# State space convolution and MLP on one core: turned products read on POOL's queue, four buffers for tile a, and a new order of the work

## The chip, the core and the metric

The program runs on one core of one Trainium2 chip. The core has five engines: PE (matrix products), DVE (VectorE), ACT (ScalarE), POOL (GpSimd) and SP, which here only issues transfers. Each engine works through its own instructions in their order; semaphores join them. SP and POOL both issue DMA transfers, and sixteen DMA engines move the bytes of either. The metric is the device time of one execution in microseconds (us): before the change 343.65 us, the median of 3 runs (342.4, 343.65 and 347.39).

## The reference

With `x` of 2048 positions and 512 channels, the reference computes `h = x + A(layernorm(x))` and returns `h + B(layernorm(h))`. A is a state space layer: a kernel `K` of 2048 taps per channel is built from 128 complex exponentials, and the sequence is convolved with it through an FFT of twice the length. B normalizes once more and is a two-layer MLP of width 1376 with gelu.

```python
def _A_ref(u, A_re, A_im, B_re, B_im, C_re, C_im, log_dt, Dskip):
    ...
    P = jnp.exp(logdA[:, :, None] * l[None, None, :])
    K = jnp.einsum("dn,dnl,dn->dl", Cc, P, dB).real
    ...
    Yf = Uf * Kf[None, :, :, :]
    y = (lambda x, s, axes=(-2,-1): jnp.fft.irfft2(x, s=s, axes=axes).astype(jnp.bfloat16))(Yf, (1, L2), axes=(-2, -1))[:, :, 0, :L]
    y = (lambda x, *d: x.transpose(*d))(y, 0, 2, 1) + u * Dskip[None, None, :]
...
x = A_u
h = x + _A_ref(_layernorm(x, axis=-1), A_A_re, A_A_im, A_B_re, A_B_im, A_C_re, A_C_im, A_log_dt, A_Dskip)
h2 = h + _B_ref(_layernorm(h, axis=-1), B_w1, B_b1, B_w2, B_b2)
```

## The kernel before

The kernel does the transforms as matrix products with tables that it makes itself, and works on the channels in two halves of 256 (`hh` is 0 or 1). Its stages, with the names that the profile shows:

- **Front.** POOL makes index rows (`si`, `ga`, `lf`, `wp`, `wq`), DVE and ACT make the layer's parameters (`psi`, `th`, `amp`, tiles `w`), ACT the sines of the tables (`M`, `base`) and the first exponentials (`Pt`, `Q`, written `<-th`). DVE takes the statistics of `x` (`st<-x`).
- **A stage** (`norm_in`): for each of 16 slices of `x` one normalized slice `u`, two products `aps<-u,BD` on PE, a cast `a<-aps` to bf16 on ACT or DVE, and a write `A_dram<-a` of 256 KB on SP. Tile `a` has two buffers. Four reads `X<-A_dram` of 1 MB each bring the result back in another order.
- **Exponentials times sines** (`p_half`, `q_half`): eight units p and ten units q for each half. A unit is a pair of products `pv` or `qv` on PE, a sine `s<-pv` or `sq<-qv` on ACT, and a product in place on DVE (`Pt<-s,Pt` or `Q<-sq,Q`).
- **Kernel taps** (`kgen`): four groups of 128 small products `kps<-Q,Pt` with as many weight loads on PE; a copy `ku` on ACT and two sums `near` and `far` on DVE after each group; then writes to `KD_near` and `KD_far` in DRAM and five reads `kt`, three on SP and two on POOL.
- **X stage** (`x_stage`): 16 units of eight products `xps<-X,M` and a cast back into `X`.
- **Convolution** (`conv`): eight steps for each half. A step is the spectrum of the taps, 22 products into `kfps` (lines 838 and 840), a cast `kf` on ACT, four DVE products `pa`, `pb`, then eight products `zps<-pa,R` on PE and a cast `z`. SP writes `z` to DRAM (`Zd<-z`, 256 KB, line 883). A read then turns it into `ZT` (`ZT<-Zd`, 256 KB in 16 rows of 16 KB, line 881). Tile `z` has three buffers, each free when its write has landed.
- **Weights** (`loads`): after the taps `kt` of the second half have come, POOL issues the loads of the MLP's weights and of `x` again (`w_r`, `w_sb`, `r`), 4.8 MB.
- **MLP** (`mlp`): it starts with four products `y<-ZT` (line 890) that need all turned products of the second half, then normalizes, and alternates `h1ps` and `o2ps` on PE with gelus on ACT to the end.

Each piece of work up to the MLP is recorded as an operation (`Sched.op`) with a list of those it depends on and a cost. A table of numbers, `ORDER`, found outside the program, says in which order the operations' instructions are written: an even number 2n is operation n on its first engine, an odd one on its second (a cast can go to ACT or DVE). The costs are not used when the program is built. So `ORDER` alone sets the order on each engine, on SP's and POOL's queues too; PSUM tiles have three buffers (`p`) and one (`q`, for `zps`). The MLP's order is that of its code.

The two lines that issue the write and the turned read of a convolution step are these:

```python
        def turn(k2=k2):
            nc.sync.dma_start(K.ZT[k2:k2 + 121:8, hh].rearrange("p h j d -> p (h j d)"), Zd[4 * k2:4 * k2 + 4].rearrange("f (q r) d -> (f q) (r d)", q=4))

        w = S.op("SP", 0.45, lambda cell=cell, ks=ks: nc.sync.dma_start(Zd[2 * ks.start:2 * ks.stop].rearrange("f p d -> p f d"), cell["zs"][:].rearrange("p k c d -> p (k c) d")), [e], rel=[e], lat=2.4)
        K.o_z.append(S.op("SP", 0.45, turn, [w, K.o_turn], lat=2.8))
```

Of the kernel before, what the change touches and what calls it, by code (L numbers as in the profile page):

```python
# [161 lines left out]
def prefix(nc0, S, K, cp, ct, c2):  # L162
# [36 lines left out]
    K.lf = ct.tile([P, 21], f32, name="lf")  # L199
    at = 0  # L200
    for base, n in ((256, 2), (511, 4), (1022, 7), (2044, 4), (1, 4)):
        count(nc0, K.lf[:, at:at + n], base, [[1, n]])
        at += n
# [487 lines left out]
def kgen(nc, S, K, cv, sc, psp, hh, KD):  # L691
# [40 lines left out]
    def gets():  # L732
        kt = K.kt[hh] = cv.tile([P, 5, HW], bf16, name="kt", tag="kt", bufs=2)
        for t in range(5):
            src = near[:].rearrange("(g k) r c -> (k r) g c", g=4)[128 * t:128 * t + 128] if t < 2 else far[t - 2].rearrange("(g k) r c -> (k r) g c", g=4)
            (nc.gpsimd if t % 2 else nc.sync).dma_start(kt[:, t, :].rearrange("p (g c) -> p g c", g=4), src)
# [431 lines left out]
```

## Time and profile before

| what | us |
|---|---|
| median of 3 runs | 343.65 |
| the profiled execution's own time | 341.9 |
| its span, first to last instruction | 340.1 |
| PE busy in the span | 253.5 |
| DVE busy | 203.8 |
| ACT busy | 188.0 |
| POOL busy | 32.6 |

The profile is of one execution. Times within it count from the start of its span; the 1.8 us between span and own time lie around it. A busy PE is not PE at its peak, since products overlap. In the tables by stretch, the columns are the stretch, its length, then for PE, PE's weight loads, DVE, ACT and POOL the busy time with the number of instructions in brackets, then the granted PE clock (1.00 is full), the busy share of the DMA engines and GB/s. SPq is SP's queue, "PEld" are weight loads, "issue" is time in which an engine waited for nothing that the profile shows.

### The profile page before, as it was taken

What the parts mean: (1) busy time and instruction counts of PE and PEld (TensorE: products, weight loads), DVE (VectorE), ACT (ScalarE), POOL (GpSimd) and SP (SyncE); (2) the same over time, 40 slices, a digit from 0 to 9 for tenths busy, and PEclk for the clock granted to TensorE, in tenths of its full rate; (3) what the DMA queues carried; (4) which work ended last, traced back from release to release, by engine and by line L of the source; (5) the groups of instructions that cost most, each with busy time, mean ns of one, the idle gap of its engine ahead of it and who ended that gap; (6) DMA issues with size and microseconds to landing.
All of it is one profiled execution on the core that took longest, in us unless ns stands there. A gap on an engine that the chain in (4) does not pass through costs nothing.

```text
span 340.1 us, 6070 instructions
## 1 busy us (share of the span) xinstructions
PE 253.5 (75%) x2408; PEld 155.3 (46%) x2422; DVE 203.8 (60%) x427; ACT 188.0 (55%) x308; POOL 32.6 (10%) x92
## 2 busy tenths in 40 slices
PE   4046984476674998998798978502689799999996
PEld 4012351242373775667666755401465344444443
DVE  3999995559981999989224443510727367274102
ACT  2799796479832999986143525420573263363440
POOL 8200007800000100000015000100000000000000
PEclk9655567579955899999599997965599999999999
DMA  6400007640156921111098964443000100100001
GB/s 180 175 2 0 4 18 195 201 147 0 65 166 169 245 67 31 45 49 35 4 239 225 337 230 125 123 124 93 0 2 0 46 17 15 47 2 31 31 11 52
DMA packets 29830, 30.18 MB, mean 89 GB/s; under 512 B 7113, under 2 KB 27594, under 8 KB 29418
## 3 DMA queue, kind: packets, MB, share of 16 engines
q1 hardware_dynamic: 27722, 23.03, 23.4%
q0 software_dynamic: 2080, 6.76, 6.4%
q8 instruction: 19, 0.31, 0.4%
q14 instruction: 9, 0.07, 0.1%
HBM read 18.58 MB, written 11.20 MB: 88 GB/s over the span
## 4 chain that ended last, share of the span: by engine, by line
PE 36%; DMA 24%; DVE 18%; ACT 12%; issue 6%; POOL 2%; SPq 1%; DVEq 0%; ACTq 0%; POOLq 0%
DMA Zd<-z 13%; PE h1ps L992 12%; PE o2ps L1004 9%; PE kps L704 5%; DMA A_dram<-a 5%; PE kfps L840 4%; DMA kt<-KD_far 3%; DVE st L761 3%; DVE Pt L70 3%; DMA KD_far<-far 2%; DVE w L70 2%; ACT a L80 2%; PE yps L974 2%; ACT y2T L80 2%; DVE Q L70 1%
## 5 line engine op out<-in xcount | busy, mean ns | idle before, releaser
L994 ACT ACTIVATE hT<-h1ps,b_sb 128x512 bf16<-128x512 f32 (+3 forms) x55 | 33.0, 603 | 28.0 <-PE h1ps L992 27.4
L992 PE MATMUL h1ps<-y2T,w_r 128*128 128x512 bf16 (+3 forms) x217 | 44.7, 350 | 2.3 <-ACT y2T L80 1.9
L840 PE MATMUL kfps<-kt,M 128*128 128x256 bf16 x320 | 42.2, 278 | 1.2 <-DMA kt<-KD_far 0.6
L1004 PE MATMUL o2ps<-w_sb,hT 128*128 128x512 bf16 (+3 forms) x183 | 39.2, 366 | 1.7 <-DVE ot L70 1.5
L840 PEld LDWEIGHTS <-M 128*128 128x128 bf16 x320 | 29.2, 99 | 10.1 <-issue 3.4
L992 PEld LDWEIGHTS <-w_r 128*128 128x128 bf16 (+1 forms) x220 | 23.0, 105 | 22.4 <-issue 4.9
L70 DVE TENSOR_TENSOR pa<-X,kf 128x1024 bf16<-128x1024 bf16 x16 | 11.1, 691 | 28.1 <-ACT kf L80 28.1
L1004 PEld LDWEIGHTS <-hT 128*128 128x128 bf16 (+1 forms) x187 | 18.1, 98 | 20.9 <-issue 1.8
L704 PE MATMUL kps<-Q,Pt 128*32 128x20 bf16 x1024 | 18.6, 221 | 11.2 <-issue 9.6
L70 DVE TENSOR_TENSOR ot<-o2ps,h_sb 128x512 bf16<-128x512 f32 (+1 forms) x13 | 8.4, 650 | 29.6 <-PE o2ps L1004 28.7
L80 ACT CAST kf<-kfps 128x1024 bf16<-128x1024 f32 x14 | 14.2, 1013 | 17.2 <-PE kfps L840 9.0
L704 PEld LDWEIGHTS <-Pt 128*32 128x32 bf16 x1024 | 17.9, 169 | 12.4 <-issue 10.5
L80 ACT CAST z<-zps 128x1024 bf16<-128x1024 f32 x15 | 15.3, 1023 | 13.6 <-DMA Zd<-z 12.8
L80 ACT CAST a<-aps 128x1024 bf16<-128x1024 f32 x15 | 15.0, 1033 | 12.2 <-DMA A_dram<-a 12.2
L70 DVE TENSOR_TENSOR Pt<-s,Pt 128x1024 bf16<-128x1024 bf16 x32 | 20.4, 691 | 1.2 <-ACT s L118 1.1
L118 ACT ACTIVATE sq<-qv 128x1024 bf16<-128x1024 int16 x20 | 20.3, 1072 | 0.0
L613 ACT ACTIVATE Pt<-th 128x256 bf16<-128x256 f32 x64 | 20.3, 405 | 0.0
L80 ACT COPY y2T<-tps 128x512 bf16<-128x512 bf16 x16 | 8.5, 584 | 17.6 <-PE tps L984 17.6
L405 POOL DMA_DIRECT2D Dp<-Dd x24 | 13.0, 546 | 43.7 <-DMA Dd<-ds 42.1
L70 DVE TENSOR_TENSOR h_sb<-yps,r 128x512 f32<-128x512 f32 x12 | 8.3, 689 | 14.8 <-PE yps L974 14.8
L777 PE MATMUL aps<-u,BD 128*128 128x512 bf16 x30 | 11.0, 473 | 8.0 <-DVE u L772 5.3
L118 ACT ACTIVATE s<-pv 128x1024 bf16<-128x1024 int16 x16 | 16.6, 1064 | 0.0
(224 smaller groups left out, 470.9 us busy)
## 6 DMA issues: line engine op xcount, KB each, us to landing
A_dram<-a SPq DMA_DIRECT2D x16, 256.0 KB, 3.0
X<-A_dram SPq DMA_DIRECT2D x4, 1024.0 KB, 6.0
Zd<-z SPq DMA_DIRECT2D x16, 256.0 KB, 3.4
ZT<-Zd SPq DMA_DIRECT2D x16, 256.0 KB, 3.4
...
out_dram<-ot SPq DMA_DIRECT2D x15, 128.0 KB, 1.7
...
```

Of the source, the lines that this page charges most:

```text
L70: nc.vector.tensor_tensor(out, a, b, op)
L80: nc.scalar.copy(out, in_)
L118: nc.scalar.activation(out, v.bitcast(i16)[..., 0:2 * n:2], ACT.Sin, scale=S2PI / 65536)
L405: nc.gpsimd.dma_start(t[o::128 // cnt], bass.AP(row.tensor, row.offset + 1024 * kh, [[0, cnt], [1, 1024]]))
L613: nc.scalar.activation(K.Pt[:, k, 1, :], K.th[:, ds], ACT.Exp, scale=float(8 * k))
L704: nc.tensor.matmul(kps[32 * g:32 * g + 32, i // 8, at:at + 20], lhsT=Pt[:, :, u, c], rhs=Q[:, :, u, c], start=True, stop=True, tile_positi ...
L761: o = S.op("DVE", 2.9, roots, deps=[S.op("DVE", 0.62, lambda j=j: nc.vector.bn_stats(st[:, j, :], x[:, j, :]), [here]) for j in range(16)])
L777: nc.tensor.matmul(ps[:, h, :], lhsT=K.BD[:, h].rearrange("p a b -> p (a b)"), rhs=cell["u"][:], start=True, stop=True)
L840: nc.tensor.matmul(ps[:, k, c, :], lhsT=K.M[:, t, 2 * k2 + k, c, :], rhs=kt[:, t, :], start=(c == 1 and t == 0), stop=(t == 4))
L992: nc.tensor.matmul(pt[:fs, 0:n], lhsT=K.w1_sb[:, dc, fc * P:fc * P + fs], rhs=y2T[tb][:, dc, js, :].rearrange("p a b -> p (a b)"), start=( ...
L994: nc.scalar.activation(hT[tb % 2][:fs, fc, cols], pt[:fs, 0:n], ACT.Gelu_apprx_tanh, bias=K.b1_sb[:fs, fc:fc + 1], scale=1.0)
L1004: nc.tensor.matmul(pt[:], lhsT=h[:fs, fc, jj * P:(jj + 1) * P], rhs=K.w2_sb[:fs, fc, d], start=(fc == 0), stop=(fc == NFC - 1))
```

## The change

The turned reads `ZT<-Zd` go out on POOL's queue instead of SP's. Tile `a` gets four buffers instead of two. The small rows for the table phases are made differently: POOL makes three rows `si` in f32 instead of six in bf16, and five small ACT instructions turn them, `ga` and `kf` into the bf16 rows, where DVE made three of these before; `lf` is made earlier on POOL. The bookkeeping of the operations is extended: a transfer is now two operations, its issue on SP or POOL and a "DMA" operation that issues nothing, so operation numbers shift. The costs are changed, which the built program doesn't use. `ORDER` is another table: the new numbers give another order on PE, ACT, DVE, POOL and SP up to the end of the convolution. The MLP is untouched.

```diff
 ORDER = [
-    106, 250, 0, 2, 20, 22, 4, 24, 26, 16, 192, 30, 28, 36, 34, 38, 144, 32, 62, 140, 40, 148, 152, 64, 156, 278, 82, 272, 44, 84, 268, 138, 274, 54, 276, 108, 258, 126, 252,
+    110, 4, 24, 28, 8, 32, 38, 6, 40, 196, 36, 136, 126, 124, 66, 132, 112, 42, 148, 68, 122, 138, 134, 22, 114, 130, 128, 116, 168, 304, 120, 70, 140, 118, 144, 164, 290,
...
+    def dma(self, eng, cost, fn, deps, size, rel=(), acq=None, lat=2.2):
+        i = self.op(eng, cost, fn, deps, acq)
+        return self.op("DMA", size, None, [i], None, rel, lat)
...
-    si = c2.tile([1, 6, P], bf16, name="si")
+    si = c2.tile([1, 3, P], f32, name="si")
+    sb = c2.tile([1, 2, 3, P], bf16, name="sb")
...
+        count(nc0, si[:, n], 1, pattern)
         for m in range(2):
-            count(nc0, si[:, 2 * n + m], 1 - 128 * m, pattern)
-            R[nm + "m" * m] = si[:, 2 * n + m]
+            R[nm + "m" * m] = sb[:, m, n]
...
-    ts(nc, R["k"][:], kf[0:1, :], 1.0 / 128, ALU.mult)
-    for m, div in enumerate((8192, 64)):
-        ts(nc, gb[:, m], ga[:], 1.0 / div, ALU.mult)
-    K.o_rows = S.op("DVE", 0.4, nc.vector.split(nc0.vector), [K.o_bits])
+
+    def rows():
+        nc0.scalar.activation(R["k"][:], kf[0:1, :], ACT.Copy, scale=1.0 / 128)
+        for m, div in enumerate((8192, 64)):
+            nc0.scalar.activation(gb[:, m], ga[:], ACT.Copy, scale=1.0 / div)
+        for m in range(2):
+            nc0.scalar.activation(sb[:, m], si[:], ACT.Copy, bias=-128.0 * m)
...
         def out(e, cell=cell):
-            cell["a"] = lp.tile([P, 2, 512], bf16, name="a", tag="a", bufs=2)
+            cell["a"] = lp.tile([P, 2, 512], bf16, name="a", tag="a", bufs=4)
             evac(nc, e, cell["a"][:], cell["p"][:])
...
         def turn(k2=k2):
-            nc.sync.dma_start(K.ZT[k2:k2 + 121:8, hh].rearrange("p h j d -> p (h j d)"), Zd[4 * k2:4 * k2 + 4].rearrange("f (q r) d -> (f q) (r d)", q=4))
+            nc.gpsimd.dma_start(K.ZT[k2:k2 + 121:8, hh].rearrange("p h j d -> p (h j d)"), Zd[4 * k2:4 * k2 + 4].rearrange("f (q r) d -> (f q) (r d)", q=4))
```

What the new table moves is shown at three places. The first is SP's queue from the end of the taps of the second half on. `Zd0` and `Zd1` are the two halves' products in DRAM, `z_...` the buffers. Before:

```order
L729 DMA KD_near1_67<-near_2304 128x512
L730 DMA KD_far1_66<-far_2305 128x3x256
L881 DMA ZT_2585<-Zd0_68 16x8192 x2
L883 DMA Zd0_68<-z_2627 128x4x256
L736 DMA kt_2656<-KD_near1_67 128x4x64
L736 DMA kt_2656<-KD_far1_66 128x4x64 x2
L881 DMA ZT_2585<-Zd0_68 16x8192
L883 DMA Zd0_68<-z_2686 128x4x256
L881 DMA ZT_2585<-Zd0_68 16x8192
L883 DMA Zd0_68<-z_2770 128x4x256
L881 DMA ZT_2585<-Zd0_68 16x8192
L883 DMA Zd1_69<-z_2814 128x4x256
```

SP's queue after, from the same place:

```order
L741 DMA KD_near1_67<-near_2145 128x512
L742 DMA KD_far1_66<-far_2146 128x3x256
L895 DMA Zd0_68<-z_2580 128x4x256
L895 DMA Zd0_68<-z_2617 128x4x256
L748 DMA kt_2620<-KD_near1_67 128x4x64
L748 DMA kt_2620<-KD_far1_66 128x4x64 x2
L895 DMA Zd0_68<-z_2686 128x4x256
L895 DMA Zd0_68<-z_2770 128x4x256
L895 DMA Zd1_69<-z_2814 128x4x256
L895 DMA Zd1_69<-z_2858 128x4x256
```

Before, every write stands behind the read of the write ahead of it; after, only writes and the taps' transfers are left. The reads now stand on POOL's queue, around the taps `kt` of the second half and the loads of the weights. POOL after:

```order
L748 DMA kt<-KD_near_65 128x4x64
L748 DMA kt<-KD_far_64 128x4x64
L893 DMA ZT<-Zd_68 16x8192 x4
L748 DMA kt<-KD_near_67 128x4x64
L748 DMA kt<-KD_far_66 128x4x64
L893 DMA ZT<-Zd_68 16x8192 x2
L1131 COPY gate<-kt 128x1
L932 DMA w_r_2697<-in_B_w_dram 128x4x1376
```

POOL after, from the last of the weights' loads on:

```order
L1136 DMA r_2709<-in_A_u_dram 128x6144
L1137 CAST b_sb<-b_bf 128x11
L893 DMA ZT<-Zd_68 16x8192 x2
L893 DMA ZT<-Zd_69 16x8192 x8
L959 MEMSET hT_3109 1x512
```

Four turned reads of the first half stand ahead of the two taps' reads that POOL issues; the last two of the first half and all of the second stand behind the loads.

The second place is SP's queue around the taps of the first half. Before:

```order
L798 DMA X<-A_dram 128x8x512
L418 DMA M<-Bd 1x64x128 x2
L798 DMA X<-A_dram 128x8x512
L729 DMA KD_near_65<-near 128x512
L730 DMA KD_far_64<-far 128x3x256
L798 DMA X<-A_dram 128x8x512
L736 DMA kt<-KD_near_65 128x4x64
L736 DMA kt<-KD_far_64 128x4x64 x2
L798 DMA X<-A_dram 128x8x512
```

SP after:

```order
L810 DMA X<-A_dram 128x8x512 x4
L741 DMA KD_near_65<-near 128x512
L742 DMA KD_far_64<-far 128x3x256
L430 DMA M<-Bd 1x64x128 x2
L748 DMA kt<-KD_near_65 128x4x64
L748 DMA kt<-KD_far_64 128x4x64 x2
```

All four reads of X now stand ahead of the taps' writes. The third place is ACT from the A stage into the sines of the first half (`a<-aps` are the A stage's casts, `u` its normalized slices, `s` and `sq` the sines, `ku` the copy after a group of kernel taps). Before:

```order
L80 CAST a<-aps 128x1024
L586 CAST M<-w_210 128x32x16
L501 CAST M<-psi_202 128x16x32
L80 CAST a<-aps 128x1024 x4
L770 ACTIVATE u<-x,mv,r1y 128x512
L80 CAST a<-aps 128x1024
L118 ACTIVATE s<-pv 128x1024 x2
L118 ACTIVATE sq<-qv 128x2x32x16
```

ACT after:

```order
L80 CAST a<-aps 128x1024
L118 ACTIVATE s<-pv 128x1024
L598 CAST M<-w_208 128x32x16
L118 ACTIVATE s<-pv 128x1024 x3
L782 ACTIVATE u<-x,mv,r1y 128x512
L80 CAST a<-aps 128x1024
L80 COPY QL<-lps 128x2048
L118 ACTIVATE s<-pv 128x1024
L118 ACTIVATE sq<-qv 128x2x32x16
L118 ACTIVATE sq<-qv 128x8x8x16
L118 ACTIVATE sq<-qv 128x2x32x16 x4
L118 ACTIVATE sq<-qv 128x8x8x16
```

Before, eleven of ACT's fifteen casts `a` stand ahead of the first sine `s`; after, three of its nine do, and the rest lie between the sines. DVE makes seven of the sixteen casts after, one before.

More of the change, by code (lines that the diff above doesn't have):

```diff
@@ L179, in prefix @@
     count(nc0, kf[:], 0, [[1, 64]])
+    K.lf = ct.tile([P, 21], f32, name="lf")
+    at = 0
+    for base, n in ((256, 2), (511, 4), (1022, 7), (2044, 4), (1, 4)):
+        count(nc0, K.lf[:, at:at + n], base, [[1, n]])
+        at += n
+    start = S.op("POOL", 2.6, None)
     K.ones = cp.tile([P, P], bf16, name="ones")
@@ L198, in prefix @@
             R[f"{nm}{1 << n}"] = gb[:, m, n]
[L199 to L203, printed above, removed]
+    table = S.op("POOL", 2.6, None, [start])
     split = ((3, 15), (0, 7), (0, 1), (1, 1), (4, 1))
@@ L226, in prefix @@
     K.bw = bw
-    K.o_bits = S.op("DVE", 1.6, nc.vector.split(nc0.vector))
+    K.o_bits = S.op("DVE", 1.5, nc.vector.split(nc0.vector), [start])
     R["k"] = c2.tile([1, 64], bf16, name="row_k")
-    ts(nc, R["k"][:], kf[0:1, :], 1.0 / 128, ALU.mult)
-    for m, div in enumerate((8192, 64)):
-        ts(nc, gb[:, m], ga[:], 1.0 / div, ALU.mult)
-    K.o_rows = S.op("DVE", 0.4, nc.vector.split(nc0.vector), [K.o_bits])
+    def rows():
[4 more added lines that the diff above has]
+            nc0.scalar.activation(sb[:, m], si[:], ACT.Copy, bias=-128.0 * m)
+    K.o_rows = S.op("ACT", 1.5, rows, [table])
     mask = c2.tile([P, 8], bf16, name="mask")
@@ L267, in outer @@
             count(nc, wq[p0:p1, at:at + cnt], base, pattern + [[0, 2]])
-    pl = S.op("POOL", 6.0, lambda: None)
+    pl = S.op("POOL", 4.4, None, [K.o_rows])
     def make():
@@ L389, in tables @@
     d = S.op("DVE", 1.35, dirichlet, [f])
-    w = S.op("SP", 0.7, lambda: nc.sync.dma_start(Dd[:].rearrange("r p l -> p r l"), ds[:].rearrange("p a r l -> p (a r) l")), [d], lat=2.5)
+    w = S.dma("SP", 0.55, lambda: nc.sync.dma_start(Dd[:].rearrange("r p l -> p r l"), ds[:].rearrange("p a r l -> p (a r) l")), [d], 0.3)
     b = S.op("DVE", 1.5, last_row, [f])
-    wb = S.op("SP", 0.7, lambda: nc.sync.dma_start(Bd[:].rearrange("r p l -> p r l"), bs[:].rearrange("p t c l -> p (t c) l")), [b], lat=2.5)
+    wb = S.dma("SP", 0.55, lambda: nc.sync.dma_start(Bd[:].rearrange("r p l -> p r l"), bs[:].rearrange("p t c l -> p (t c) l")), [b], 0.3)
     sums = []
@@ L411, in mul @@
                        cell["t"][:].rearrange("p (k b f) -> p k b f", k=8, f=k2), ALU.mult)
-            x = S.op("POOL", 2.0 if n < 4 else 7.0, spread, [w] + K.o_free, acq=DT[n], lat=2.5)
-            sums.append(S.op("DVE", 1.23, mul, [x, bases[n, 0]] + K.o_src, rel=[x]))
+            x = S.dma("POOL", 1.1 if n < 4 else 4.4, spread, [w] + K.o_free, 0.8, acq=DT[n])
+            sums.append(S.op("DVE", 1.23, mul, [x, bases[n, 0]] + K.o_src, rel=[x - 1]))
     def put_rows():
@@ L418, in put_rows @@
             nc.sync.dma_start(K.M[127:128, 1:5, :, c, :], Bd[c:8:2].rearrange("t (k h) l -> t k (h l)", k=16).unsqueeze(0))
-    K.o_tab = S.op("SP", 1.4, put_rows, sums + [wb, K.o_m[1]], lat=2.5)
+    K.o_tab = S.dma("SP", 1.4, put_rows, sums + [wb, K.o_m[1]], 0.2)
     S.group = "turned"
@@ L455, in tr @@
                 T[nm] = ps[:, n, :]
-        arrive = S2("LOAD", 0.85, lambda: None, [arrive] if arrive is not None else [])
+        arrive = S2("LOAD", 0.85, None, [arrive] if arrive is not None else [])
         Z[pair[0]] = S2("PE", 1.75, tr, [arrive], acq="p", bias=300)
@@ L717, in out @@
                     stt(nc, o[:, :, d], v[:, a, :], K.half_sign[:], cell["u"][:, a], ALU.mult, ALU.add)
-            m = S.op("PE", 2.6, mms, K.o_p[s] + K.o_q[s], acq="p")
+            m = S.op("PE", 2.15, mms, K.o_p[s] + K.o_q[s], acq="p")
             mm.append(m)
@@ L736, in gets @@
             (nc.gpsimd if t % 2 else nc.sync).dma_start(kt[:, t, :].rearrange("p (g c) -> p g c", g=4), src)
-    p = S.op("SP", 2.0, puts, ends, rel=[ends[0]], lat=3.0)
-    K.o_kt[hh] = S.op("SP", 1.0, gets, [p], lat=3.0, acq="kt")
+    p = S.dma("SP", 1.4, puts, ends, 0.6, rel=[ends[0]], lat=2.4)
+    K.o_kt[hh] = S.dma("SP", 1.6, gets, [p], 0.6, acq="kt", lat=2.6)
 def norm_in(nc, S, K, lp, psp, x, A_dram):
@@ L758, in roots @@
         stt(nc, mv[:, :, 1], mv[:, :, 0], -1.0, K.rs[:], ALU.mult, ALU.mult)
-    here = S.op("XLOAD", 13.5, lambda: None)
+    here = S.op("XLOAD", 13.5, None)
     o = S.op("DVE", 2.9, roots, deps=[S.op("DVE", 0.62, lambda j=j: nc.vector.bn_stats(st[:, j, :], x[:, j, :]), [here]) for j in range(16)])
@@ L785, in norm_in @@
         a = S.op(("ACT", "DVE"), (0.94, 1.2), out, [m], acq="a", rel=[m])
-        K.o_a.append(S.op("SP", 0.7, lambda cell=cell, j=j: nc.sync.dma_start(A_dram[:, :, j, :], cell["a"][:]), [a], rel=[a], lat=2.5))
+        K.o_a.append(S.dma("SP", 0.55, lambda cell=cell, j=j: nc.sync.dma_start(A_dram[:, :, j, :], cell["a"][:]), [a], 0.78, rel=[a]))
 def x_load(nc, S, K, A_dram, change, gate):
@@ L798, in load @@
             nc.sync.dma_start(K.X[:].rearrange("p k c d -> p (k c) d")[:, ks], av[:, ks])
-        K.o_xl.append(S.op("SP", 1.0 if n else 1.2, load, K.o_xl[-1:] if n else K.o_a + gate, lat=3.5 + 2.5 * n))
+        K.o_xl.append(S.dma("SP", 0.5, load, [K.o_xl[-1] - 1] if n else K.o_a + gate, 2.95))
 def x_stage(nc, S, K, psp, hh):
@@ L871, in conv @@
         S.group = f"kf{hh}"
-        p = S.op("PE", 4.8, spectrum, [K.o_kt[hh], K.o_tab, K.o_m[1], K.o_top, K.o_r] + [K.o_x[hh][k2]] + back_ops[max(k2 - 2, 0):k2 - 1], acq="p", rel=[K.o_kt[hh]], bias=-1.0 * k2)
+        p = S.op("PE", 4.8, spectrum, [K.o_kt[hh], K.o_tab, K.o_m[1], K.o_top, K.o_r] + [K.o_x[hh][k2]] + back_ops[max(k2 - 2, 0):k2 - 1], acq="p", rel=[K.o_kt[hh] - 1], bias=-1.0 * k2)
         f = S.op(("ACT", "DVE"), (1.0, 1.2), out, [p], acq="kf", rel=[p], bias=-1.0 * k2)
@@ L880, in turn @@
         def turn(k2=k2):
-            nc.sync.dma_start(K.ZT[k2:k2 + 121:8, hh].rearrange("p h j d -> p (h j d)"), Zd[4 * k2:4 * k2 + 4].rearrange("f (q r) d -> (f q) (r d)", q=4))
-        w = S.op("SP", 0.45, lambda cell=cell, ks=ks: nc.sync.dma_start(Zd[2 * ks.start:2 * ks.stop].rearrange("f p d -> p f d"), cell["zs"][:].rearrange("p k c d -> p (k c) d")), [e], rel=[e], lat=2.4)
-        K.o_z.append(S.op("SP", 0.45, turn, [w, K.o_turn], lat=2.8))
+            nc.gpsimd.dma_start(K.ZT[k2:k2 + 121:8, hh].rearrange("p h j d -> p (h j d)"), Zd[4 * k2:4 * k2 + 4].rearrange("f (q r) d -> (f q) (r d)", q=4))
+        w = S.dma("SP", 0.5, lambda cell=cell, ks=ks: nc.sync.dma_start(Zd[2 * ks.start:2 * ks.stop].rearrange("f p d -> p f d"), cell["zs"][:].rearrange("p k c d -> p (k c) d")), [e], 0.85, rel=[e])
+        K.o_z.append(S.dma("POOL", 0.65, turn, [w, K.o_turn], 1.0))
 def first_half(nc, K, out, hh, js):
@@ L1084, in change @@
         K.X = xp.tile([P, 16, 2, 512], bf16, name="X")
-    S = Sched({"p": PB, "q": QB, "kf": 2, "z": 3, "pa": 2, "s": 4, "ko": 2, "ku": 1, "u": 2, "a": 2, "kt": 2})
+    S = Sched({"p": PB, "q": QB, "kf": 2, "z": 3, "pa": 2, "s": 4, "ko": 2, "ku": 1, "u": 2, "a": 4, "kt": 2})
     def part(group, fn, *args):
@@ L1128 @@
     K.o_turn = S.op("NONE", 0.0, turn, K.o_kgen)
-    ld = S.op("POOL", 6.0, loads, [K.o_kt[1]], lat=8.0)
+    ld = S.op("POOL", 6.0, loads, [K.o_kt[1]])
+    for n in range(4):
+        S.op("DMA", 3.0, None, [ld])
     part("kf0", conv, cv, psp, Zd[0], 0)
```

30 rows, old and new, of the table ORDER are left out of this document.

## The prediction

> **What bounds the kernel now.** I read the table by stretch first, cut where the chain of waits changes its owner.
>
> ```profile
> 0.00:56.00 56.00, 31.11 (x114) 14.52 (x116) 48.65 (x123) 42.06 (x86) 12.91 (x56) 0.66 0.24 72
> 56.00:73.00 17.00, 9.28 (x45) 5.19 (x46) 7.14 (x12) 8.87 (x11) 9.76 (x20) 0.51 0.66 199
> 73.00:92.30 19.30, 12.46 (x73) 5.36 (x73) 18.38 (x32) 18.45 (x21) 0.00 (x0) 1.00 0.10 34
> 92.30:109.40 17.10, 10.49 (x518) 9.78 (x519) 9.10 (x19) 4.47 (x7) 0.00 (x0) 0.53 0.62 179
> ...
> 204.30:220.30 16.00, 12.06 (x84) 8.24 (x83) 6.85 (x13) 6.99 (x8) 0.98 (x2) 0.89 0.48 132
> 220.30:236.10 15.80, 0.00 (x0) 0.00 (x0) 1.95 (x5) 2.49 (x3) 0.00 (x0) 0.58 0.42 117
> 236.10:340.10 104.00, 92.56 (x496) 48.67 (x503) 47.51 (x121) 42.94 (x74) 0.00 (x0) 0.94 0.06 21
> ```
>
> Three stretches stand out in which no engine is full. In 56 to 73 DVE works 7.14 of 17 us and ACT 8.87. In 92.3 to 109.4 the kernel taps run on PE at half clock. In 220.3 to 236.1 PE does nothing at all. The last 104 us are the MLP, whose code and order the change leaves alone.
>
> The groups of the costliest instructions say what the first gap is: ACT's casts `a` wait for the write of `A_dram` that still holds one of the two buffers.
>
> ```profile
> L80 ACT CAST a<-aps 128x1024 bf16<-128x1024 f32 x15 | 15.0, 1033 | 12.2 <-DMA A_dram<-a 12.2
> ```
>
> The third gap shows in the timeline of SP's queue, the chain of waits and SP's waits. The first number of each row is its start.
>
> ```profile
> 204.28 0.48 SPq L881 DMA_DIRECT2D ZT<-Zd  x1
> 204.85 0.53 SPq L883 DMA_DIRECT2D Zd<-z  x1
> ...
> 229.29 0.57 SPq L883 DMA_DIRECT2D Zd<-z  x1
> 232.83 0.48 SPq L881 DMA_DIRECT2D ZT<-Zd  x1
> ```
>
> ```profile
> 185.49 11.74 DMA Zd<-z
> ...
> 232.83 3.07 DMA ZT<-Zd
> ...
> 236.15 1.03 PE y L890 x4
> ```
>
> ```profile
> SPq L881 <- DMA Zd<-z: 41.5, 11, 11.4
> ```
>
> Each turned read stands on SP until the write ahead of it has landed, and the next write stands behind that read although its data lie ready. So SP makes one step per round trip. ACT shows how far it falls behind:
>
> ```profile
> 190.92 1.01 ACT L80 CAST kf<-kfps 128x1024 bf16<-128x1024 f32 x1 [1.76 <-issue]
> 194.61 1.01 ACT L80 CAST kf<-kfps 128x1024 bf16<-128x1024 f32 x1 [1.76 <-issue]
> 204.34 1.01 ACT L80 CAST z<-zps 128x1024 bf16<-128x1024 f32 x1 [5.03 <-DMA Zd<-z]
> 220.30 1.01 ACT L80 CAST z<-zps 128x1024 bf16<-128x1024 f32 x1 [3.00 <-DMA Zd<-z]
> ```
>
> Undisturbed, a step takes 194.61 - 190.92 = 3.69 us. The last four take (220.30 - 204.34) / 4 = 3.99. The last cast ends at 221.31, and its write goes out at 229.29, 7.98 us later.
>
> **The turned reads on POOL.** SP now holds only writes there, so the last one goes out as its cast ends: 7.98 us fall away. What comes late next is PE's own step, 3.69 instead of 3.99: another 4 x 0.30 = 1.2. The stall of 5.03 us at 204.34 is a wait for a buffer whose write stood behind a read; but that write shared the DMA engines with the weights, and it still queues behind the one of 185.49, which took 11.74 us. So between nothing and all 5.03 of it goes, and with PE running ahead meanwhile I take 1.0. That makes 2.2 for the steps, between 1.2 and 6.2.
>
> POOL's reads are not in this trace. Nearest are the reads of the taps, issued by both engines (size of one, median us to landing):
>
> ```profile
> ZT<-Zd SPq DMA_DIRECT2D x16, 256.0 KB, 3.4
> ...
> kt<-KD_far SPq DMA_DIRECT2D x4, 64.0 KB, 6.5
> ...
> kt<-KD_far POOLq DMA_DIRECT2D x2, 64.0 KB, 4.7
> ```
>
> ```profile
> L405 POOL DMA_DIRECT2D Dp<-Dd x24 | 13.0, 546 | 43.7 <-DMA Dd<-ds 42.1 <-DMA Dp<-Dd 1.0 <-issue 0.4
> ...
> L736 POOL DMA_DIRECT2D kt<-KD_far x2 | 1.5, 753 | 0.3 <-issue 0.3
> ```
>
> POOL's issue takes 0.55 to 0.75 us against SP's 0.48. Only the last read is exposed. I charge 0.5 for it, the issue and a wake; the bounds are a loss of 1.3 and a gain of 1.8, the difference between 6.5 and 4.7. The Trainium skill, page "DMA: Bandwidth & Descriptors", section "Latency and other measured facts", gives a first byte after about 1 us from GpSimd and 0.6 us from SP; by that the charge would be an estimated 0.4. POOL's own queue: the last reads stand behind the weights' loads, issued once the taps are there; each waits for its own write only, so they are late only while the loads last. Behind them stand only memsets that the MLP's second layer needs. End of the convolution: 7.98 + 2.2 - 0.5 = 9.7 us.
>
> **Four buffers and the order, up to the taps of the first half.** DVE is busy 48.65 + 7.14 + 18.38 + 9.10 = 83.3 of the first 109.4 us, ACT 73.9. Two groups of DVE's instructions price what the order moves:
>
> ```profile
> L70 DVE TENSOR_TENSOR M<-base,Dp 128x1024 bf16<-128x1024 bf16 x12 | 7.5, 700 | 0.0
> ...
> L82 DVE COPY QL<-lps 128x2048 bf16<-128x2048 bf16 x2 | 2.5, 1226 | 2.0 <-PE lps L517 2.0
> ```
>
> The new order gives DVE six more casts `a`, about 1.2 us each like the casts `kf` shown below, and takes the two copies `QL` and about ten shorter instructions from it; I take that as balanced, an estimate good to 2 us, and ACT gets as much as DVE loses, some 5. In 73 to 92.3, where sines and products alternate, DVE reaches 18.38 / 19.30 = 95%. The casts that now wait in 56 to 73 move between the sines, and four buffers cover four of the writes. If the first 56 us stay and the remaining 34.65 us of DVE run at 95%, DVE ends at 56 + 36.5 = 92.5. The kernel taps come behind that:
>
> ```profile
> 99.62 1.13 issue
> 100.75 2.32 PE kps L704 x127
> 103.07 4.70 issue
> ...
> 109.40 3.07 DMA KD_far<-far
> 112.49 6.46 DMA kt<-KD_far
> 118.99 1.03 PE kfps L840 x8
> ```
>
> A group takes 2.32 and then 1.13 us in which PE has no instructions. Three groups follow the last product that they need, 10.4 us, with ten products M (6.3) and the sums queued on DVE beside them, some 8: 2 more, 94.5. One gap grew to 4.70, and it lies under the reads of X:
>
> ```profile
> 98.12 0.37 SPq L798 DMA_DIRECT2D X<-A_dram  x1
> 100.09 0.45 SPq L798 DMA_DIRECT2D X<-A_dram  x1
> 110.61 0.49 SPq L798 DMA_DIRECT2D X<-A_dram  x1
> ...
> 98.00:106.50 8.50, 3.94 (x227) 3.73 (x220) 2.73 (x8) 1.01 (x3) 0.00 (x0) 0.50 0.88 243
> ```
>
> That reads as instructions that come by DMA and queue with the 2 MB (243 GB/s over 8.5 us). All four reads of X now go out together, over the last groups, so one or two gaps of 4.70 come instead of 1.13. With one and a half, 5.4 us, the last `far` comes at 100 where it was 109.3. The rows' bounds are 92.5 and 109: a gain between nothing and 17.
>
> **From there to the convolution of the second half.** ACT sets the pace: a table load and the exponentials, then the sines.
>
> ```profile
> 108.62 1.28 ACT L620 ACT_TABLE_LOAD   x1
> ...
> 130.00 1.02 ACT L118 ACTIVATE s<-pv 128x1024 bf16<-128x1024 int16 x1
> ...
> 124.29 1.23 DVE L82 CAST kf<-kfps 128x1024 bf16<-128x1024 f32 x1 [0.31 <-PE kfps L840]
> ```
>
> Those 21.4 us stay, and one cast `kf` now stands ahead of the first sine: a gain of 9.3 becomes 8. The cover for it is thin. Between the last cast `a` and the last `far` lie on DVE the same ten products, two products Pt and the sums, some 10 us, so that cast ends near 84.5 and the reads of X start near 88; four of them take 2 x 8.4 us, to 105. Seven casts X on DVE (1.2 each, as the `kf` cast) and two spectra (118.99 to 124.29, 5.3 us) end at 119, just ahead of ACT at 122. Sines and casts are as many as before, so the second half's taps begin 8 us earlier; one spectrum, 2.65 us, now stands between their groups. The convolution of the second half starts 5.4 us earlier. SP's taps no longer wait behind three turned reads; I count that at nothing, since PE has spectra to do meanwhile. The rows for the tables on ACT are five instructions in a time when ACT waits for parameters anyway; without that cover they cost about 1.5.
>
> **The sum.** 5.4 + 9.7 = 15.1 us off the profiled execution's 341.9: 326.8. The median of the runs lies 1.75 above that execution, which is within their spread; I say 327. What can be told from no change is about 2%, 6.9 us.
>
> **The rivals.** *The front gives nothing* (0.17). For it: the first 56 us have DVE at 87% and end the same chain; the coupling of ACT and DVE may eat what the gap gives. Then 341.9 - 9.7 = 332.
>
> *The front gives all* (0.12): instruction fetches don't collide, and the stall of 5.03 goes too. 12 + 9.7 = 22 off: 320. Against it speaks that X now lies over three groups.
>
> *Only the issue time goes* (0.06): writes and reads fill the same DMA engines, and the reads on POOL delay the writes as much as SP's order did. Then eight issues of 0.48 are saved, 3.8 us, and with the front 341.9 - 5.4 - 3.8 = 333. The Trainium skill, page "DMA: Bandwidth & Descriptors", section "Issuing engines are not separate DMA queues", states this: issuing from several engines saves only the sequencer's time. The trace bears out the shared engines, but not that they are full here: the DMA share in 204.3 to 220.3 is 0.48, and SP waits 41.5 us with nothing to do.
>
> *X as one block* (0.07), the slower side. Place: SP's queue between the last write of `A_dram` and the taps of the first half. The first sine of the second half can't come before the start of X plus 16.8 + 8.5 + 5.3 + 1.0 = 31.6 us. Now X starts at 98.12 and that sine at 130.00, so the block costs from the point where X starts later than 98.4. It can: twelve casts `a` now lie between the sines, where both engines are 95% full; if the sines don't begin before 73, X starts near 73 + 19.3 + 13 + 3 = 108, and near 112 with a few waits more. At 112 the sum is 341.9 + 13.6 + 2.65 - 9.7 = 348. Against it: the 17 us in which both engines idle are there to be used.
>
> The forecast keeps 0.58. The range takes in the forecast with its bounds and the two cases beside it: 317 (front 12 and end 13) to 337 (front nothing, end 6). The chances: faster by over 2%, below 336.8, in nearly all of the forecast and most of the first three rivals, 0.86; within 2%, 0.10; slower by over 2%, part of the last rival, 0.04.
>
> **What would show it.** Right: SP's writes of the second half follow their casts within 1 us; PE idles less than 9 us before `y`; the casts `a` no longer wait for `A_dram`, and the first sine comes before 65; the last `far` near 100, with gaps over 3 us between the `kps` groups. Wrong: the last turned read lands more than 5 us after its write; ACT's casts `z` wait on at the steps' end; or X starts after 98.

## The result, and the profile after

The kernel after takes 323.02 us, the median of 4 runs (320.75 to 326.27), where the kernel before took 344.7 beside it. The ratio is 0.9346, with a 95% interval of 0.9227 to 0.9466. The profiled execution took 320.75 us with a span of 319.0, which is 21.1 us off the span of 340.1. In five of the experiments below (two buffers, X split, `r` behind the fourth read, and both runs of the two small edits) the profiled execution was over 1.5% above that kernel's fastest, and so were three of the four executions of X split, so that times read from these profiles can lie some us late and X split has no interval.

Lines of the changed kernel have higher numbers: the turned read is L893 (L881 before), the write `Zd<-z` L895, the reads of X L810, the write `KD_far` L742, the reads `kt` L748, the products `y` L902. The table by stretch of the kernel after, cut at its own marks, has the columns as before: the stretch, its length, busy time of PE, PE's weight loads, DVE, ACT and POOL, the granted PE clock, the DMA share and GB/s.

```profile
54.10:86.10 32.00, 23.70 (x443) 13.57 (x448) 29.98 (x51) 29.51 (x33) 11.07 (x22) 0.98 0.52 165
86.10:95.60 9.50, 3.40 (x181) 3.10 (x175) 5.41 (x11) 0.48 (x1) 0.00 (x0) 0.50 0.90 286
...
173.10:208.70 35.60, 31.67 (x252) 23.21 (x251) 16.61 (x33) 16.53 (x18) 10.03 (x19) 0.99 0.89 272
208.70:215.40 6.70, 0.16 (x1) 0.00 (x0) 2.63 (x5) 1.48 (x2) 1.94 (x4) 0.50 0.43 117
215.40:319.00 103.60, 91.77 (x496) 48.29 (x503) 47.50 (x121) 42.74 (x74) 0.00 (x0) 0.95 0.06 21
```

From the first sine on, at 54.1, DVE is busy 29.98 of 32.0 us: the stretch in which both engines had idled is gone. The stretch before `y`, in which PE stands still, is 6.7 us long where it was 15.8. The MLP takes 103.6 us where it took 104.0.

The groups of the casts `a` in the kernel after show that nearly nothing waits for `A_dram` any more; the first number behind the second bar is the idle time ahead, 12.2 us on ACT before.

```profile
L80 ACT CAST a<-aps 128x1024 bf16<-128x1024 f32 x9 | 9.0, 1026 | 0.5 <-PE aps L789 0.4
L82 DVE CAST a<-aps 128x1024 bf16<-128x1024 f32 x7 | 8.5, 1220 | 0.3 <-PE aps L789 0.3
```

The timeline of the kernel after at the end of the convolution: the last cast, its write, the last two reads and the products that need them.

```profile
207.67 1.01 ACT L80 CAST z<-zps 128x1024 bf16<-128x1024 f32 x1 [2.27 <-issue]
208.70 0.36 SPq L895 DMA_DIRECT2D Zd<-z  x1
209.53 0.48 POOL L893 DMA_DIRECT2D ZT<-Zd  x1 [4.11 <-DMA Zd<-z]
211.51 0.48 POOL L893 DMA_DIRECT2D ZT<-Zd  x1 [1.50 <-DMA Zd<-z]
215.45 1.87 PE L902 MATMUL y<-ZT,Dm 128*128 128x256 bf16 x8 [6.59 <-issue]
```

The write goes out 0.02 us after its cast ends at 208.68, where it stood 7.98 us behind. The chain of waits of the kernel after has these pieces that the rest speaks of; the numbers are start and length.

```profile
88.94 13.10 DMA X<-A_dram
...
106.67 2.59 issue
109.34 0.56 ACT X L80
...
161.65 8.14 DMA KD_far<-far
...
170.33 2.74 DMA kt<-KD_far
173.11 0.92 PE kfps L852 x7
...
181.16 13.55 DMA Zd<-z
```

The marks of both profiles side by side:

| mark | before | after | gain |
|---|---|---|---|
| first sine of the first half | 73.03 | 54.12 | 18.9 |
| first read of X issued | 98.12 | 86.14 | 12.0 |
| last copy `ku` of the first half | 108.18 | 95.64 | 12.5 |
| first sine of the second half | 130.00 | 120.31 | 9.7 |
| last copy `ku` of the second half | 168.84 | 159.96 | 8.9 |
| `kfps` that waited for the far taps | 180.68 | 173.11 | 7.6 |
| last cast `z` ends | 221.31 | 208.68 | 12.6 |
| products `y` | 236.15 | 215.45 | 20.7 |

So the front brings 7.6 us, the steps of the second half 5.1, and what follows the last cast 8.1 (14.84 us shrink to 6.77).

### The profile page after: what moved, and what is told of

It reads as the page before. It is cut to its first block, busy times and chain, and to the rows that moved or that the text cites. A ratio compares the mean times of both kernels' runs of the same rounds, so it can differ in the third digit from the quotient of the medians.

```text
span 319.0 us, 6069 instructions
## 1 busy us (share of the span) xinstructions
PE 250.1 (78%) x2408; PEld 154.0 (48%) x2422; DVE 204.6 (64%) x420; ACT 193.4 (61%) x317; POOL 38.6 (12%) x105
## 4 chain that ended last, share of the span: by engine, by line
PE 43%; ACT 18%; DMA 17%; DVE 13%; issue 8%; SPq 1%; ACTq 0%; DVEq 0%; POOLq 0%
PE h1ps L1004 12%; PE o2ps L1016 10%; PE kfps L852 6%; DMA Zd<-z 5%; DMA X<-A_dram 4%; PE kps L716 4%; ACT sq L118 3%; DVE st L773 3%; DMA KD_far<-far 3%; ACT s L118 3%; DMA A_dram<-a 2%; DVE w L70 2%; ACT Pt L625 2%; PE v L341 2%; PE yps L986 2%
## 5 line engine op out<-in xcount | busy, mean ns | idle before, releaser
L1004 PE MATMUL h1ps<-y2T,w_r 128*128 128x512 bf16 (+3 forms) x217 | 43.9, 346 | 2.7 <-ACT y2T L80 1.9
L852 PE MATMUL kfps<-kt,M 128*128 128x256 bf16 x320 | 40.7, 274 | 0.7 <-DMA kt<-KD_far 0.7
L80 ACT CAST kf<-kfps 128x1024 bf16<-128x1024 f32 x15 | 15.2, 1014 | 20.0 <-issue 10.7
L118 ACT ACTIVATE sq<-qv 128x1024 bf16<-128x1024 int16 x20 | 19.4, 1079 | 0.0
L417 POOL DMA_DIRECT2D Dp<-Dd x24 | 12.6, 529 | 44.1 <-DMA Dd<-ds 43.7
L893 POOL DMA_DIRECT2D ZT<-Zd x16 | 7.8, 491 | 81.1 <-ACT ku L720 56.0
L688 PE MATMUL qv<-RQ,QL 128*128 128x128 bf16 (+1 forms) x61 | 11.0, 294 | 5.2 <-ACT sq L118 2.4
```

Of the source, the lines that this page charges most:

```text
L80: nc.scalar.copy(out, in_)
L118: nc.scalar.activation(out, v.bitcast(i16)[..., 0:2 * n:2], ACT.Sin, scale=S2PI / 65536)
L417: nc.gpsimd.dma_start(t[o::128 // cnt], bass.AP(row.tensor, row.offset + 1024 * kh, [[0, cnt], [1, 1024]]))
L688: nc.tensor.matmul(v[:, n], lhsT=K.QL[:, b + n, :], rhs=K.RQ[:, m0:m1].rearrange("p i c d -> p (i c d)"), start=True, stop=True)
L852: nc.tensor.matmul(ps[:, k, c, :], lhsT=K.M[:, t, 2 * k2 + k, c, :], rhs=kt[:, t, :], start=(c == 1 and t == 0), stop=(t == 4))
L1004: nc.tensor.matmul(pt[:fs, 0:n], lhsT=K.w1_sb[:, dc, fc * P:fc * P + fs], rhs=y2T[tb][:, dc, js, :].rearrange("p a b -> p (a b)"), start=( ...
```

## The experiments

**The queue of the reads, in the new order and in the old.** Two kernels take the move apart. The first is the kernel after with the reads back on SP:

```diff
-            nc.gpsimd.dma_start(K.ZT[k2:k2 + 121:8, hh]...
+            nc.sync.dma_start(K.ZT[k2:k2 + 121:8, hh]...
```

> The kernel after, with the turned reads back on SP's queue and everything else as it is, the new order too. Theory (reads and writes block each other in SP's row): SP's last write waits again for the landing of writes ahead of it, so that PE idles 14 to 17 us before the products y instead of 6.6, and the time rises by 8 to 13 us, to 331 to 336 (ratio to the kernel before 0.96 to 0.975). Rival (only the issue time of a queue is saved): eight issues of 0.48 us come back, at most 4 us, a ratio of 0.936 to 0.946.

Measured: 323.95 us, a ratio of 0.9443 (0.9385 to 0.9501), so the rival's range. Of 21 us only some 2 to 3 are lost, and the interval overlaps that of the kernel after. In the profile `y` comes 1.9 us later, and 1.0 of these are there at the first sine of the second half already (121.29), ahead of the first turned read. SP's queue at the end, in this kernel, shows why:

```profile
203.28 0.48 SPq L893 DMA_DIRECT2D ZT<-Zd  x1
203.81 4.03 SPq L895 DMA_DIRECT2D Zd<-z  x2
207.88 1.15 SPq L893 DMA_DIRECT2D ZT<-Zd  x2
211.31 0.36 SPq L895 DMA_DIRECT2D Zd<-z  x1
211.72 2.37 SPq L893 DMA_DIRECT2D ZT<-Zd  x2
```

The last cast ends at 211.28 and its write goes out at 211.31, from SP's queue with the reads in it. In the new order a read stands one or two writes behind its own, so its data have nearly landed when SP reaches it, and the last write stands behind no long wait. From the last cast to `y` it is 6.04 us. My expectation named the queue, and it was the order.

The second is the kernel before with the reads on POOL and nothing else (the same line, `sync` to `gpsimd`).

> The kernel before, with nothing changed but the queue of the turned reads: POOL instead of SP, in the old order and with two buffers for a. Theory: the end of the convolution gains alone what it gains in the whole change, 10 to 13 us, so 332 to 335, a ratio of 0.962 to 0.971, and SP's last write follows its cast within 1 us. Rival (only the issue time): about 4 us, a ratio of 0.989. Second rival (the move pays only in an order made for it, since five reads now stand on POOL ahead of the taps' reads kt): nothing or a loss, a ratio of 1.00 or more, with kt of the second half landing later than 184.

Measured: 333.96 us, 0.9735 (0.968 to 0.9791), a gain of 9 us, a little short of the theory's 10 to 13. The theory holds in kind: the last cast ends at 222.91, its write goes out at 222.93, and from that cast to `y` it is 7.59 us. The second rival is right in part. POOL issued its reads `kt` behind five turned reads, and the far taps came late in this kernel:

```profile
172.30 2.44 POOL L881 DMA_DIRECT2D ZT<-Zd  x5 [55.90 <-ACT ku L708]
176.25 0.79 POOL L736 DMA_DIRECT2D kt<-KD_near  x1 [1.51 <-DMA KD_near<-near]
182.24 0.77 POOL L736 DMA_DIRECT2D kt<-KD_far  x1 [5.20 <-DMA KD_far<-far]
```

From the write `KD_near` at 172.63 to the spectra at 184.53 it took 11.9 us, where the kernel before took 9.6 (171.10 to 180.68).

**Reads shifted on SP.** If the place in the row is what counts, POOL isn't needed. In the kernel before, the last two turned reads of the first half and those of the second half, but for the very last, move behind the next write; SP keeps them all. The table of numbers changes so that SP has this order (an extract):

```diff
 L883 DMA Zd1_69<-z
-L881 DMA ZT<-Zd1_69
 L883 DMA Zd1_69<-z
+L881 DMA ZT<-Zd1_69
```

> The kernel before, with all reads on SP's queue and nothing changed but their place there: each turned read of the second half, and the last two of the first, stand one write further back, behind the next write instead of ahead of it. Theory (what cost the end of the convolution was a write standing behind a read that waits, not the queue that issues it): the last write follows its cast within 2 us, PE's wait before y falls from 16.6 to 9 us or less, and 7 to 9 us of the 9 that POOL's queue gave come without POOL, a ratio of 0.972 to 0.980. Rival (it needs a second queue): 2 us at most, 0.994 or more.

Measured: 330.93 us, 0.9652 (0.9602 to 0.9703), 12 us, above what the theory gave and, with intervals that overlap, above what POOL's queue gave. The timeline of this kernel, the rows of the casts, of SP and of `y`:

```profile
214.06 1.02 ACT L80 CAST z<-zps 128x1024 bf16<-128x1024 f32 x1
...
215.10 0.36 SPq L883 DMA_DIRECT2D Zd<-z  x1
...
215.56 0.48 SPq L881 DMA_DIRECT2D ZT<-Zd  x1
...
217.35 1.01 ACT L80 CAST z<-zps 128x1024 bf16<-128x1024 f32 x1 [2.27 <-issue]
...
218.38 0.36 SPq L883 DMA_DIRECT2D Zd<-z  x1
218.84 2.32 SPq L881 DMA_DIRECT2D ZT<-Zd  x2
...
224.38 1.87 PE L890 MATMUL y<-ZT,Dm 128*128 128x256 bf16 x8 [6.24 <-DMA ZT<-Zd]
```

Each of the last four writes goes out within 0.05 us of its cast's end, and from the last cast to `y` it is 6.02 us. This settles it: a write that stood behind a waiting read cost the end of the convolution, and both a second queue and another place in the same queue remove that.

**Four buffers, in the old order and taken from the new.** The kernel before with four buffers:

```diff
-            cell["a"] = lp.tile([P, 2, 512], bf16, name="a", tag="a", bufs=2)
+            cell["a"] = lp.tile([P, 2, 512], bf16, name="a", tag="a", bufs=4)
```

> The kernel before, with four buffers for a instead of two and nothing else changed. Theory (buffers and order each bring a part): the 12.2 us that ACT's casts a wait for A_dram mostly go, but DVE then sets the pace, so the last far comes 3 to 5 us earlier than 109.3 and the time falls by about 4, a ratio of 0.988. Rival (the buffers are all of the front's gain): 8 us, a ratio of 0.977. Rival (only the order brings it): no change, 1.00.

Measured: 333.83 us, 0.9753 (0.9694 to 0.9811): 8.5 us, the first rival's number and twice the theory's. ACT's casts wait 2.6 us for `A_dram`, not 12.2; the first sine comes at 65.10 (73.03), the last `ku` at 99.99 (108.18), the first sine of the second half at 122.25 (130.00), `y` at 227.92 (236.15). The 8 us gained by 65 arrive whole at the end. Now the kernel after with two buffers (the same line, 4 to 2):

> The kernel after, with two buffers for a instead of four and the rest as it is. Theory (the new order spreads the casts among the sines, and then few of them have to wait): 3 to 5 us more than the kernel after, a ratio to the kernel before of 0.945 to 0.950. Rival (the buffers carry the front's gain): 8 us or more, a ratio of 0.958 or above. Rival (the order does it alone): 0.935 as after.

Measured: 330.68 us, 0.9638 (0.9571 to 0.9704), behind the kernel after by 0.026 to 0.029, 9 to 10 us; the first rival again. The groups of the casts in this kernel:

```profile
L80 ACT CAST a<-aps 128x1024 bf16<-128x1024 f32 x9 | 9.1, 1023 | 4.6 <-DMA A_dram<-a 3.5 <-PE aps L789 1.1
L82 DVE CAST a<-aps 128x1024 bf16<-128x1024 f32 x7 | 8.6, 1222 | 6.2 <-DMA A_dram<-a 6.2
```

Spread among the sines, the casts wait nearly as long as before, 9.7 us together on `A_dram` where it was 12.2, and now a waiting cast holds up sines and products. X is first read at 93.40 instead of 86.14, and the first sine of the second half comes at 127.46, 34.1 us behind it. The new order needs the four buffers.

**Both small edits in the old order.** The kernel before with four buffers and the reads on POOL, run twice, the second time beside the unchanged kernel after.

> The kernel before with the two small edits together, four buffers for a and the turned reads on POOL, in the old order and with the rows as before. Alone they gave ratios of 0.9753 and 0.9735. Theory (front and end are separate places, and their gains add): 1 - 0.0247 - 0.0265 = 0.949, so 0.944 to 0.954, and what is left to the kernel after, some 5 us, is what the new order brings. Rival (the new order is not needed): 0.935 as after. Rival (one gain is taken back where the other is made, the taps' reads on POOL behind five turned reads): 0.960 or more.

> The kernel after itself, unchanged, beside the next one on the same chip. It gave a ratio of 0.9346 and should give it again, 0.928 to 0.942.

> Again the kernel before with four buffers for a and the turned reads on POOL in the old order, which gave 0.9392 with an interval of 0.928 to 0.951. Theory (the new order brings little of its own, since the old one with the two small edits already frees both places): within 3 us of the kernel after, a ratio of 0.933 to 0.944. Rival (the gains only add up and the order brings the rest, 5 us): 0.946 to 0.952.

Measured: 326.07 us, 0.9392 (0.9278 to 0.9505), and again 326.75, 0.945 (0.9371 to 0.9529), beside 322.9, 0.9382 (0.9321 to 0.9444), of the kernel after. Together the two edits give about what they gave apart (0.0247 + 0.0265 makes 0.949), perhaps a little more. The first value lies between the theory and the first rival of its expectation, the second just outside the theory and just short of the rival, so neither expectation was met. What is left for the new order is, in the runs side by side, 0.945 - 0.938 = 0.007 or 2.4 us; the intervals overlap, so its size stays open. The rows for the tables on ACT are in this rest; they were not tried alone.

**The four reads ahead of the taps.** In the kernel after, the first four turned reads move on POOL behind the reads of the second half's taps. POOL's order:

```diff
-L893 DMA ZT<-Zd_68 16x8192 x4
 L748 DMA kt<-KD_near_67 128x4x64
 L748 DMA kt<-KD_far_66 128x4x64
+L893 DMA ZT<-Zd_68 16x8192 x4
```

> The kernel after, with the first four turned reads of the first half moved on POOL behind the taps' reads of the second half instead of ahead of them. Theory (the four reads, 1 MB, delay the write KD_far, which took 8.14 us against 4.71 before): KD_far lands in 5 us or less, the spectra of the second half start 3 us earlier, near 170, and the time falls by about 3, a ratio to the kernel before of 0.926. Rival (the reads only move their load onto the writes Zd, which already wait beside the weights): the spectra start earlier and ACT's casts z wait as much longer, 0.935.

Measured: 330.73 us, 0.9621 (0.9547 to 0.9695): 8 to 9 us slower than the kernel after, which neither foresaw. The start is as the theory has it. POOL in this kernel:

```profile
163.58 0.75 POOL L748 DMA_DIRECT2D kt<-KD_near  x1 [59.30 <-DMA KD_near<-near]
164.90 0.75 POOL L748 DMA_DIRECT2D kt<-KD_far  x1 [0.57 <-DMA KD_far<-far]
165.64 2.44 POOL L893 DMA_DIRECT2D ZT<-Zd  x5
```

`KD_far`, issued at 162.21, has landed by 164.90. SP issues its own three reads `kt` at 166.96 to 169.8, behind two writes `Zd`, which is no later than in the kernel after (165.95 to 170.8). But they now run beside the five turned reads, and in the chain of waits the last of them takes 7.55 us, where it took 2.74. The spectra wait for them, as PE's timeline shows:

```profile
175.39 1.24 PE L852 MATMUL kfps<-kt,M 128*128 128x256 bf16 x4 [2.37 <-DMA kt<-KD_near]
176.81 1.44 PE L852 MATMUL kfps<-kt,M 128*128 128x256 bf16 x6 [0.18 <-DMA kt<-KD_far]
...
178.51 2.31 PE L852 MATMUL kfps<-kt,M 128*128 128x256 bf16 x10
...
182.52 1.26 PE L852 MATMUL kfps<-kt,M 128*128 128x256 bf16 x10
```

The table by stretch shows what that wait brings, for this kernel and then for the kernel after at the same place:

```profile
173.00:175.40 2.40, 0.03 (x2) 0.05 (x2) 1.25 (x3) 0.99 (x2) 0.00 (x0) 0.97 1.41 196
175.40:181.00 5.60, 5.35 (x23) 3.10 (x23) 0.00 (x0) 0.10 (x1) 3.43 (x7) 0.50 0.53 129
```

```profile
172.40:173.10 0.70, 0.05 (x1) 0.00 (x0) 0.67 (x3) 0.58 (x1) 0.13 (x2) 1.00 1.35 383
173.10:181.00 7.90, 7.89 (x65) 5.97 (x65) 2.97 (x7) 3.71 (x4) 5.76 (x10) 1.00 0.96 269
```

PE stood still for 2.4 us, and the granted clock was 0.50 in the 5.6 us behind. Ten products took 2.31 us, and 1.26 once the clock was back. In the kernel after PE pauses for 0.7 us there and keeps the full clock. So the spectra start 3.7 us later, and the last cast comes 7.5 us later.

**The reads of X split.** In the kernel after, two of the four reads of X go behind the writes of the first half's taps. SP's order:

```diff
-L810 DMA X<-A_dram 128x8x512 x4
+L810 DMA X<-A_dram 128x8x512 x2
 L741 DMA KD_near_65<-near 128x512
 L742 DMA KD_far_64<-far 128x3x256
+L810 DMA X<-A_dram 128x8x512 x2
```

> The kernel after, with two of the four reads of X moved on SP behind the writes of the first half's taps, as they stood before. Theory (the reads of X bind the second half's first sine, which came 34 us after the first read in the kernel after and 32 us in the kernel before): the group gap of 4.97 us shrinks below 3 and the last far comes 2 to 4 us earlier than 96.8, but the last X lands 4 to 6 us later, so the time rises by 2 to 5 us, a ratio of 0.941 to 0.950. Rival (the last far and the exponentials behind it bind): 2 to 4 us faster, 0.923 to 0.929.

Measured: 331.71 us (325.94 to 333.88, before 344.37). The fastest of the four, 325.94, is 0.946 of the kernel before, in the theory's range and 3 us above the kernel after; the other three lie 8 to 11 us above the kernel after. So the direction is the theory's, and the size stays open. The last `ku` comes at 94.98 instead of 95.64, and the gap ahead of the last group is 4.42 us, so that part of the theory fell. The third read of X goes out at 96.67, PE and behind it the casts on DVE stop for its data, and the first sine of the second half comes at 125.67 instead of 120.31:

```profile
109.09 1.22 DVE L82 CAST X<-xps 128x1024 bf16<-128x1024 f32 x1 [8.91 <-PE xps L830]
```

**The last load of the weights later.** In the kernel after, the load of `r` (1.5 MB) goes behind the fourth, then behind the last turned read of the second half:

```diff
-        nc.gpsimd.dma_start(K.r1[:], xv[:, 4:16])
+        K.late = lambda: nc.gpsimd.dma_start(K.r1[:], xv[:, 4:16])
...
             nc.gpsimd.dma_start(K.ZT[k2:k2 + 121:8, hh]...
+            if hh and k2 == LATE:
+                K.late()
```

> The kernel after, with the last of the weights' loads, the 1.5 MB of r, issued on POOL behind the fourth turned read of the second half instead of ahead of all. Theory (the writes Zd wait for the loads in the DMA engines, and through three buffers the casts z wait for the writes, 5.3 us in the kernel after): these waits fall below 3 us and the time by 2 to 3, a ratio of 0.926 to 0.930. Rival (the other loads, 3.3 MB, are enough to hold the writes up): no change, 0.935. Rival (r now comes in the way of the last writes and reads, or late for the MLP): slower, 0.94 or more.

> The kernel after, with the 1.5 MB load of r behind the last turned read on POOL's queue. With that load behind the fourth read the casts z waited 1.2 us for Zd instead of 5.3, but the last read landed 8 us after the last cast, 1.5 us more than in the kernel after, with the load still running. Theory: both now go, the products y come 1.5 us earlier still, and r lands some 10 us before the MLP's rows need it, a ratio of 0.918 to 0.925. Rival (r then comes late for the rows of the MLP, or its load holds up PE's instructions): 0.93 or more.

Measured: 319.5 us, 0.9267 (0.9173 to 0.9361), behind the fourth; 320.14, 0.9335 (0.9285 to 0.9386), behind the last: the theory's range, then the rival's. The casts `z` wait 1.2 us and 3.1 us for `Zd` instead of 5.3. Both kernels lie some 3 us below the kernel after (322.9 to 323.0), and neither interval is clear of its intervals. Behind the fourth, the gain of the casts is spent at the end, where the last read runs beside the load: `y` comes at 215.35, 8.2 us after the last cast. This is not a version that shows itself better.

## Why the prediction was right, and where it was not

The time lay in the range and by the forecast's mechanism, 4 us under the predicted 327; the profiled execution gained 21.1 us where the sum had 15.1. Both halves of the sum were too small: the 5.4 us up to the spectra of the second half became 7.6, and the 9.7 of the end became 13.1. By the steps:

**The last cast to `y`: 7.98 less 0.5.** Measured 8.1. The write follows its cast at once, and the last read lands in 3.9 us (211.51 to the start of `y` at 215.45), and from the last cast to `y` it is 6.77 us where SP's queue leaves 6.04 (below), so the charge for POOL measures 0.7 beside the 0.5 taken. But the step gave the reason as "SP now holds only writes there". The reads put back on SP in the new order leave 6.04 us, and shifted by one write in the old order 6.02. The queue was a sufficient means, not the cause; the order in the prediction's own change already took the reads out of the writes' way. The place to see it was the table itself: where the reads would have stood in SP's row.

**The steps: 2.2, between 1.2 and 6.2.** Measured 5.1, so the term was undersized. I took 1.0 of the 5.03 us stall. The groups of the casts `z` on ACT, of the kernel before and then of the kernel after, have the sum of such waits:

```profile
L80 ACT CAST z<-zps 128x1024 bf16<-128x1024 f32 x15 | 15.3, 1023 | 13.6 <-DMA Zd<-z 12.8 <-PE zps L865 0.8
```

```profile
L80 ACT CAST z<-zps 128x1024 bf16<-128x1024 f32 x15 | 15.4, 1027 | 9.1 <-DMA Zd<-z 5.3 <-issue 2.3 <-PE zps L877 1.6
```

I had left most of that stall to the weights in the DMA engines. From the `kfps` that waited for the far taps to the end of the last cast, the kernel before takes 40.63 us and the kernel after 35.57; with nothing but the reads shifted on SP, and the same weights loading, it is 36.30, and the casts wait 0.7 us. So most of this term was the row again. How the one stall of 5.03 us divides is not shown, since with the reads shifted PE ran at half clock while the weights loaded. Of the 5.3 that the kernel after keeps, the loads hold a part, since it falls to 1.2 with `r` loaded later.

**The front: last `far` near 100.** Measured 96.78, a gain of 12.5 us instead of 9.3, inside the bounds. The timelines of PE and DVE in the kernel after:

```profile
95.23 0.38 PE L716 MATMUL kps<-Q,Pt 128*32 128x20 bf16 x10 [4.97 <-issue]
```

```profile
96.37 0.41 DVE L112 SCALAR_TENSOR_TENSOR far<-kps,half_sign,ku 128x192 bf16<-128x192 f32 x1
```

Of the one and a half long gaps that I charged at 5.4, one came, 4.97 instead of 1.13: 1.5 us less. The other 1.7 us is work that was done sooner than 94.5. Which of buffers and order brings the front was left undivided; the runs divide it. The buffers alone bring 8.5 us, and without them the new order loses 9 to 10.

**To the second half: 21.4 us on ACT, thin cover.** The cover gave way, by a little. The timelines of PE and DVE in the kernel after:

```profile
102.17 0.37 PE L827 MATMUL xps<-X,M 128*128 128x256 bf16 x1 [3.12 <-DMA X<-A_dram]
...
104.08 1.23 DVE L82 CAST X<-xps 128x1024 bf16<-128x1024 f32 x1 [3.23 <-PE xps L830]
```

X was read from 86.14, not 88, and landed by 102; ACT then stands 2.6 us ahead of its first cast `X` (the chain above). In the old order the first sine came 21.8 to 22.7 us behind the last `ku` (four buffers 22.3, POOL 22.7), in the new, with four buffers and X in one piece, 24.2 to 25.6. From the first read of X it is 34 us in the new order with and without POOL (34.2 and 34.0). So X binds there now: of the 12.5 us by which `far` came earlier, 9.7 are left at that sine, where the prediction's 9.3 became 8.

**Taps of the second half: 2.65 for a spectrum between the groups, nothing for SP.** The spectrum cost 0.8 (9.7 to 8.9). The nothing was wrong by 1.3: the write `KD_far` took longer, with four turned reads issued just ahead of it on POOL (8.14 us, the chain above), and the reads `kt` made up for a part. The chain of the kernel before at this place:

```profile
171.73 4.71 DMA KD_far<-far
...
177.20 3.99 DMA kt<-KD_far
```

That the turned reads are the cause is borne out by the kernel with the reads behind the taps, where it had landed within 2.7 us. That it should cost 3 us was my next error: the same bytes then met the taps' reads and cost more.

**The rivals.** *The front gives nothing* falls with the four buffers alone. *The front gives all* came nearest in time (320), but not by its conditions: one long gap stayed, and 5.3 us of waits, and of the front's 12.5 us at the last `ku` 7.6 were left at the spectra. *Only the issue time goes* is wrong as a forecast, but the sentence behind it needs a second look. The Trainium skill, page "DMA: Bandwidth & Descriptors", section "Issuing engines are not separate DMA queues", says that another issuing engine saves only the sequencer's time. In the new order that is so (2 to 3 us, about the rival's 3.8); in the old order the other engine saved 9 us, and most of that was not issue time but the wait of writes behind reads in one sequencer. *X as one block* has the right mechanism: the block measures 34.2 us where it had 31.6, and it sets that sine. It did not make the kernel slower than before, since X started at 86 and not past 98; with two buffers it starts at 93.4 and the kernel loses 9 to 10.

**The signs.** Of those that would show it right all came: the write 0.02 us behind its cast, PE's 6.59 us before `y`, the first sine at 54, the last `far` at 96.8, no waits for `A_dram` to speak of, and of the gaps over 3 us one. None of the others did: the last read landed 3.9 us after its write had landed, the casts wait early among the steps and not at their end, and X starts at 86.

**Left open.** The rows on ACT were not tried alone. Whether PE's long gap comes from instructions that queue with X was not isolated: it stayed at 4.4 us with half of the reads behind it. One trace speaks for it: with two buffers in the new order X is first read at 93.40, when most of the groups are done, and there the longest gap between the `kps` groups is 0.95 us. And what the new order as such brings is known only as little, 2.4 us by the middle values.
